# A planner that orders TensorE's work: a dearer change to "other" products, and wider bounds on their credit

## The chip, the cores and the metric

The kernel runs on one core of one Trainium2 chip. The metric is the device time of one execution in microseconds; lower is better. Times before the change: 2020.59, 2020.89 and 2028.12 us, median 2020.89 us. Besides these there is one profiled execution with its trace.

## The reference, cut to what matters

One block over a sequence of 2048 tokens with 512 features: six modulation rows from a condition vector, 32-head attention with heads of 16 features, then a mixer block (a token shift between two 512x512 products, and a two-layer MLP of 1792 hidden features).

```python
mod = (silu(c) @ w_mod).reshape(1, 6, 1, -1)          # sa, ca, ga, sb, cb, gb
h = layernorm(x) * (1 + ca) + sa
qkv = h @ wqkv                                          # q, k, v of 32 heads, 16 features each
p = softmax(q @ k.T * 16 ** -0.5)                       # 2048 x 2048 for each head
x = x + ga * ((p @ v) @ wo)
h = layernorm(x) * (1 + cb) + sb
# B: gelu(layernorm(h) @ w1), four feature groups shifted by +1, -1, +2, -2 tokens, @ w2, + h = x1
#    x1 + gelu(layernorm(x1) @ w3) @ w4
x = x + gb * B(h)
```

## The kernel before, in words

The kernel splits float32 operands in high and low parts, so a product of two matrices is three matmuls (lines 355, 357 and 359, the helper `mm3`). The attention is cut in 64 units: 4 chunks of 512 query tokens by 16 pairs of heads. A unit has 16 steps `s`, one for each 128 keys; each step has two rows `x = 2s` and `2s + 1`, one for each head of the pair.

TensorE has three kinds of work while the attention runs, and they use the array in three shapes:

- **rows** (mode "r"): one matmul of scores (`sc`, line 1036) beside one matmul of maxima (`mb`, line 1020), each on 64 of the array's 128 rows. ScalarE takes the exponential of `sc` (line 1032), VectorE the maximum of `mb` (line 1016), `LEAD` = 24 steps ahead. Each of the two needs a PSUM bank.
- **columns** (mode "c"): the probabilities times V (`pv`, lines 1113 and 1110), four matmuls side by side on 32 columns each. Line 1110 needs the low half of the probabilities, which GpSimd makes at line 1087.
- **other products** (mode "o"): the products of the whole array: q, k and v ahead of their use, and for each finished chunk wo, w1, w2, w3 and w4 with their transposes. Generators (`tail`, `o_fin` and others) yield one matmul at a time with its cost.

The order of all engines' instructions is fixed when the program is built. A planner, `Sched`, keeps a clock for each engine (`T["P"]` for TensorE) and adds estimated costs to it; the chip then executes each engine's list in order, and semaphores make it wait where an operand is late. The main loop (from line 1667) chooses again and again among rows, columns and other products:

- After a burst of up to `GRP` = 3 rows it works out `slack`: how long TensorE may do something else before the rows' banks and VectorE's or ScalarE's queue call for the next row. If at most `BACK` = 150 ns are left, the next row comes.
- Otherwise, with `CMIN` = 4 or more columns ready (or fewer that fit), columns come. Else other products run, one by one, until the clock reaches `stop`, which is now plus `slack`.
- Other products live on a **credit**. Each row adds half of `budget(s)`, at most up to `CTOP`; each product's cost is taken off. They run while the credit is over zero, or over `-OVER` while one of them holds a PSUM bank open. Over `CHIGH` they go on after `stop`, and a row does not start a burst. After each row the credit is lifted to `-OWE` if it is lower.
- `budget(s)` steers by a table, `DUES`, of how many us of other products are to be done by a step: 270.0 by step 505, 395.7 by step 765, 527.8 by step 1012, for instance.
- A change of mode costs `SWITCH` = 95 ns on the planner's clock, and `ENTER` = 107 ns more when rows are entered.

Chunks set what other products there are: the tail of a chunk can start only when the chunk's last unit is done, and the wo products wait for that.

Of the kernel before, what the change touches and what calls it, by code (L numbers as in the profile page):

```python
# [21 lines left out]
P = 128  # L22
# [25 lines left out]
TOLE = {"A": 500.0, "D": 500.0, "G": 800.0}  # L48
AGE = 0.2
DEBT = 3000.0  # L50
START, OVER = 1000, 1500
CROW, CCOL, CIN, CMID, COUT = 232.0, 230.0, 105.0, 95.0, 95.0
CFILL = 200.0
NSM = 7
# [28 lines left out]
XB = 4  # L83
SWITCH, ENTER = 95.0, 107.0
EARLY, STAY, BACK, GRACE = 300.0, 300.0, 150.0, 0.0
OWE, CTOP = 500.0, 5000.0
CHIGH, CMIN, CMOST, PTLOW, PLAG = 2500.0, 4, 6, 2, 1


class Sched:  # L90
# [14 lines left out]
    def to(self, mode):  # L105

        if self.mode != mode:
            self.T["P"] += SWITCH + (mode == "r") * ENTER
            self.mode = mode

    def now(self):
# [215 lines left out]
def kernel(ctx, tc, A_x, A_wqkv, A_wo, B_w1, B_w2, B_w3, B_w4, c, w_mod, out):  # L327
# [83 lines left out]
    sch = Sched()  # L411
# [509 lines left out]
    def drain(flag):  # L921
        while flag not in done:
            sch.step()

    def load_rows(t, src, pr, cs, to):
        for i in range(3):
            sch.dma(dma.dma_start, t[i + 1::4, to].bitcast(F32), src[2 * pr * DH:(2 * pr + 2) * DH, i, cs])
# [144 lines left out]
    def p_low(s):  # L1072

        p = pt[s].rearrange("p j n -> p (j n)")
        o, i = p.bitcast(F16)[:, 0::2], p.bitcast(U16)[:, 0::2]
        ready = e_exp.pop(s) + XX
        g, a = [max(sch.T[e], ready) for e in "GA"]
        if g > a + LACT:

            def half(h):  # L1080
                c = slice(h * CH, (h + 1) * CH)
                e_low[s] = XP["A"] + sch.crit("A", 690, ready, partial(act.activation, o[:, c], i[:, c], AF.Copy, scale=0.5))
            half(0)
            e_low[s] += 690 + 480
            second.append(partial(half, 1))
        else:
            e_low[s] = XP["G"] + sch.crit("G", 1345, ready, lambda: pool.tensor_scalar(  # L1087
                o, i, 0.5, 1.0, op0=OP.mult, op1=OP.mult))
# [38 lines left out]
    def ac_copy():  # L1127
        u, e = acs.pop()
        if u:
            drain(("of", u - 1))  # L1130
        ac = at.tile([P, CH], F32, name="ac", tag="ac", bufs=1)
        acc = pv.pop(u)
        e = sch.crit("A", cA(), e + PX, lambda: act.activation(ac, acc, AF.Copy))
        v_free[0] = e + XP["A"]
        sch.add(o_fin(u, ac, e + XP["A"]), 0)
# [439 lines left out]
    def budget(s):  # L1575
        if s < 0:
            return 800.0
        return min(BTOP, max([BLOW] + [(1000.0 * w - sch.spent) / (d - s) for d, w in DUES if d > s]))
# [5 lines left out]
    def before(s):  # L1584

        nu, r = divmod(s + 32, 16)
        if r == 0 and 0 < nu < NU:
            asked.append(nu)
        if asked:
            ci, pr = units[asked[0]]  # L1590
            keys = [("kq", pr // 4)] + [("q", pr // 8)] * (ci > 0)
            if r >= UWAIT:
                for key in keys:
                    drain(key)
            if all(key in done for key in keys):
                load_unit(asked.pop())
        if s in VAT:
            i = VAT.index(s)
            for kt in range(4 * i, 4 * i + 4):
                while kt not in near and ("vk", 0, kt) not in done:  # L1600
                    sch.step()
                if kt not in near:
                    sch.dma(dma.dma_start, vst[i][:, kt % 4], Vs[0, :, kt])
        if s == NS - 12:
            done.add("keys")
        if s == -12:
            unit_tiles(at, 2, dve, pool)
# [18 lines left out]
    def cols():  # L1626
        n, t = 0, sch.T["P"] + (sch.mode != "c") * SWITCH
        for y in pvs[:CMOST]:
            if n and y[0] % NKT == 0 and not y[1]:
                break  # L1630
            if col_at(y) > t + 20:
                break
            t += CCOL
            n += 1
        return n

    def fillers():
        for e in "ADG":
            sch.misc(e, max(sch.T["P"], sch.T[e]) + TOLE[e])

    def do_cols(n):
        sch.to("c")
        for y in pvs[:n]:
            if not y[1]:
                e_hi.pop(y[0])
            pv_part(*y)
        del pvs[:n]

    def do_row(x, t):
        sch.T["P"] = t  # L1650
        sch.to("r")
        late = sorted(e_exp)
        one_row(x)
        for q in late:
            if 2 * q < x - 2 * PLAG:
                p_low(q)
# [3 lines left out]
    while x < end or pvs or acs:  # L1660
        if acs:
            ac_copy()
        can = x < end
        if can:
            s, i = divmod(x, 2)
            if x == LENDS:
                sch.most = MOST
            if i == 0 and seen != s:
                seen = s
                before(s)  # L1670
                if s >= 0 and s % 16 == 0:
                    drain(("shift", s // 16))
            can = i or s < 0 or bool(pts)
        now, row, slack = sch.T["P"], False, LATE
        if can:
            need = (s >= 0) + (s + LEAD < NS)
            sch.flush(need)
            free = sorted(sm.t)
            one = free[need - 1 + 2 * (s < 0)]
            if one >= LATE:  # L1680
                one = free[need - 1]
            enter = (sch.mode != "r") * (SWITCH + ENTER)
        else:
            for q in sorted(e_exp):
                p_low(q)
            while second:
                second.pop(0)()
        nc_ = cols()
        if can:
            if sch.mode == "r" and burst < GRP:  # L1690
                slack = one - now
                row = slack <= STAY
            else:
                st = one
                for k in range(2, GRP + 1):
                    if need * k <= len(free) and free[need * k - 1] < LATE:
                        st = max(st, free[need * k - 1] - (k - 1) * CROW)
                dry = sch.T["D"] if s + LEAD < NS else sch.T["A"]
                slack = max(st, dry - CROW - PX - EARLY) - enter - now
                row = slack <= BACK and (sch.mode == "r" or sch.credit < CHIGH and not (nc_ >= CMIN and len(pts) <= PTLOW))  # L1700
        if not row:
            n = 0
            if nc_ >= CMIN or nc_ and slack >= nc_ * CCOL + (sch.mode != "c") * SWITCH:
                do_cols(nc_)
                n = nc_
            else:
                stop = now + max(slack, 0.0) + GRACE
                while (sch.T["P"] < stop or sch.credit > CHIGH) and sch.credit > (-OVER if sch.open else 0.0) and sch.one():
                    n += 1
            if not n:  # L1710
                if not can or one - enter > now + 100.0:
                    sch.T["P"] = now + 50.0
                else:
                    row = True
        if row:
            do_row(x, max(now, one - enter))
            burst = 1 if enter else burst + 1
            x += 1
            sch.credit = max(min(sch.credit + budget(s) / 2, CTOP), -OWE)
        fillers()  # L1720
        if tp[0] is None and x >= 2 * (NS // NC + TPO) and (x >= 2 * (NS // NC + TPL) or all(key in done for key in KEYS)):
            for key in KEYS:
                drain(key)
            qpx.close()
            tpx = ExitStack()
            tp[0] = tpx.enter_context(tc.tile_pool(name="tp", bufs=1, side="right"))
# [43 lines left out]
```

## Time and profile before

| What | Value |
|---|---|
| profiled execution: its own time | 2020.83 us |
| profiled execution: span from first to last instruction | 2019.0 us |
| mean granted TensorE clock | 0.992 |
| first and last matmul of scores | 96.02 and 1858.85 us |
| busy share: TensorE (PE) / VectorE (DVE) / ScalarE (ACT) / GpSimd (POOL) | 97% / 83% / 74% / 82% |
| instructions of the maxima at line 1016, mean | 2048, 683 ns |

In the profile PE is TensorE's matmuls and PEld its weight loads; DVE, ACT and POOL are VectorE, ScalarE and GpSimd. Matmuls are pipelined and their ends are modelled, so two that overlap by their durations may still be as close as they can be: pauses of TensorE are read from start to start. A table of stretches shows the busy us of each engine with the number of instructions in parentheses.

### The profile page before, as it was taken

To read this page: it belongs to the slowest core of one execution; us is meant where nothing else is said; L and a number is where in the kernel's file an instruction comes from. 1 tells how busy PE (TensorE), PEld (TensorE's weight loads), DVE (VectorE), ACT (ScalarE), POOL (GpSimd) and SP (SyncE) were. 2 spreads that over 40 slices of the span, in tenths; PEclk is the share of its full clock that TensorE was granted. 3 is DMA by queue.
4 is the path that set the end of the run, shared out by engine and by line. 5 is a ranking of instruction groups with operands and counts; after the bars stand their busy time and mean duration, and the time that the engine had idled before them with its cause. 6 is when DMAs were issued, how large, how long until landed. Compare 5 with 4: busy or idle time off the path is not lost.

```text
span 2019.0 us, 42344 instructions
## 1 busy us (share of the span) xinstructions
PE 1958.0 (97%) x14480; PEld 1133.0 (56%) x14480; DVE 1676.2 (83%) x3010; ACT 1495.4 (74%) x3113; POOL 1652.2 (82%) x1585
## 2 busy tenths in 40 slices
PE   7999999999999999999999999999999999998899
PEld 4655665554455555554455555555555555553798
DVE  7878888888988888889889988889998888883643
ACT  5376888888978877778787867777787777778443
POOL 6377999999989888889889988888899988887532
PEclk8999999999999999999999999999999999999999
DMA  5665878777523343435234243335333334342332
GB/s 181 203 200 164 243 230 262 253 224 258 183 86 110 114 135 123 132 111 157 77 103 143 86 142 95 115 105 195 87 102 126 106 118 135 110 133 82 141 152 89
DMA packets 233083, 293.24 MB, mean 145 GB/s; under 512 B 125876, under 2 KB 178052, under 8 KB 216580
## 3 DMA queue, kind: packets, MB, share of 16 engines
q1 hardware_dynamic: 232868, 290.53, 45.3%
q8 instruction: 115, 1.88, 0.4%
q14 instruction: 100, 0.82, 0.1%
HBM read 225.81 MB, written 62.91 MB: 143 GB/s over the span
## 4 chain that ended last, share of the span: by engine, by line
PE 76%; DVE 13%; ACT 5%; POOL 2%; issue 2%; DMA 1%; SPq 1%; POOLq 0%; ACTq 0%; DVEq 0%
PE mb L1020 14%; PE sc L1036 11%; PE pv L1113 10%; DVE mx L1016 9%; PE w L355 8%; PE w L359 7%; PE w L357 7%; PE pv L1110 7%; ACT pt L1032 2%; POOL pt L1087 1%; PE ot L1145 1%; PE v L355 1%; PE xT L1223 1%; PE q L355 1%; PE v L357 1%
## 5 line engine op out<-in xcount | busy, mean ns | idle before, releaser
L1016 DVE TENSOR_REDUCE mx<-mb 128x1 f32<-128x512 f32 x2048 | 1295.7, 683 | 160.9 <-PE mb L1020 126.2
L1087 POOL TENSOR_SCALAR pt<-pt 128x1024 f16<-128x1024 uint16 x964 | 1281.3, 1362 | 126.1 <-ACT pt L1032 122.7
L1032 ACT ACTIVATE pt<-sc 128x512 int32<-128x512 f32 x2048 | 1100.0, 608 | 312.3 <-PE mb L1020 228.3
L1020 PE MATMUL mb<-kst,qtl 64*128 64x512 f32 x2048 | 733.5, 448 | 22.1 <-DVE mx L1016 7.9
L1036 PE MATMUL sc<-qtl,kst 64*128 64x512 f32 x2048 | 709.5, 441 | 6.1 <-DMA qtl<-nm 2.3
L1020 PEld LDWEIGHTS mb<-kst,qtl 64*128 64x128 f32 x2048 | 343.5, 192 | 196.8 <-DVE mx L1016 69.7
L1036 PEld LDWEIGHTS sc<-qtl,kst 64*128 64x128 f32 x2048 | 334.5, 185 | 137.6 <-issue 48.1
L1113 PE MATMUL pv<-pt,vst 128*32 128x512 f16 x4096 | 362.5, 393 | 0.2
L1110 PE MATMUL pv<-pt,vst 128*17 128x512 f16 (+1 forms) x2048 | 215.5, 399 | 4.0 <-POOL pt L1087 4.0
L1113 PEld LDWEIGHTS <-vst 128*32 128x32 bf16 x4096 | 116.5, 94 | 117.5 <-issue 67.2
L355 PE MATMUL w<-A,wr 128*128 128x256 f32 (+2 forms) x576 | 174.6, 303 | 2.0 <-ACT pt L1032 1.3
L1447 POOL TENSOR_TENSOR g<-xs,g 128x256 fp32r<-128x256 f32 (+2 forms) x144 | 103.0, 716 | 86.1 <-ACT g L1446 83.9
L357 PE MATMUL w<-A,wr 128*128 128x256 f32 (+2 forms) x576 | 171.9, 298 | 0.5 <-DVE A L345 0.3
L359 PE MATMUL w<-A,wr 128*128 128x256 f32 (+2 forms) x576 | 171.8, 298 | 0.0
L1110 PEld LDWEIGHTS <-vst 128*17 128x17 f16 (+1 forms) x2048 | 54.0, 90 | 144.2 <-issue 135.1
L355 PEld LDWEIGHTS w<-A,wr 128*128 128x128 f32 x576 | 110.1, 191 | 30.4 <-issue 16.7
L359 PEld LDWEIGHTS w<-A,wr 128*128 128x128 f32 x576 | 109.9, 191 | 22.7 <-issue 22.7
L357 PEld LDWEIGHTS w<-A,wr 128*128 128x128 f32 x576 | 110.0, 191 | 20.6 <-issue 19.3
L355 PE MATMUL w<-wr,g 128*128 128x512 f32 x288 | 120.8, 419 | 0.7 <-ACT g L1446 0.6
L359 PE MATMUL w<-wr,g 128*128 128x512 f32 x288 | 119.1, 413 | 0.2 <-POOL g L1447 0.2
L357 PE MATMUL w<-wr,g 128*128 128x512 f32 x288 | 118.5, 412 | 0.0
L1443 ACT ACTIVATE sq<-w 128x256 f32<-128x256 f32 (+2 forms) x144 | 56.2, 391 | 56.6 <-PE w L359 54.6
(150 smaller groups left out, 2119.1 us busy)
## 6 DMA issues: line engine op xcount, KB each, us to landing
wr<-Ws SPq DMA_DIRECT2D x80, 1024.0 KB
kst<-Ks SPq DMA_DIRECT2D x189, 256.0 KB
vst<-Vs SPq DMA_DIRECT2D x252, 192.0 KB
qtl<-Qs SPq DMA_DIRECT2D x192, 64.0 KB
Vs<-vt SPq DMA_DIRECT2D x32, 384.0 KB
Ws<-wq SPq DMA_DIRECT2D x40, 256.0 KB
Ws<-wst SPq DMA_DIRECT2D x40, 256.0 KB
wst<-in_B_w_dram SPq DMA_DIRECT2D x36, 256.0 KB
```

Source lines behind the costliest of these rows:

```text
L355: te.matmul(o, lh, rh, start=first, stop=False)
L357: te.matmul(o, lh, rl, start=False, stop=False)
L359: te.matmul(o, ll, rh, start=False, stop=last)
L1016: end = sch.crit("D", 605, e + PX, lambda: dve.reduce_max(mxs[u][:, j, g, c:c + 1], b, axis=AX.X))
L1020: return ready, lambda: te.matmul(b, lhs, kst[u % 3][r, c * CH:(c + 1) * CH], start=True, stop=True), after
L1032: ea = sch.crit("A", 480, e + PX, lambda: act.activation(pt[s][:, j], b, AF.Exp))
L1036: return ready, lambda: te.matmul(b, kst[u % 3][r, kt * P:(kt + 1) * P], qst[u][r], start=True, stop=True), after
L1087: e_low[s] = XP["G"] + sch.crit("G", 1345, ready, lambda: pool.tensor_scalar(o, i, 0.5, 1.0, op0=OP.mult, op1=OP.mult))
L1110: te.matmul(acc[r:r + n, :], v[:, (kt + i) % 4, c - n:c].bitcast(F16), pt[s + i].bitcast(F16)[:, j, 0::2], start=False, stop=kt == NKT - 2 ...
L1113: te.matmul(acc[r:r + 32, :], v[:, kt % 4, r:r + 32], pt[s].bitcast(F16)[:, j, 1::2], start=kt == 0, stop=False, skip_group_check=True)
L1443: sch.chain(("A", cA(n), lambda: act.activation(sq, b, AF.Square, scale=2.0)), ("D", cD(n), cube), ("A", cA(n), lambda: act.activation(sq, ...
L1447: ("G", cG(n), lambda: pool.tensor_tensor(lo, xs, hi, op=OP.subtract)), (None, 0, end), bank=b)
```

## The change

The planner now counts 202 ns instead of 95 ns for each change to other products (rows have always cost 202, columns still cost 95). `OVER` goes from 1500 to 3000 ns, `OWE` from 500 to 1500, `CTOP` from 5000 to 7000 and `CHIGH` from 2500 to 6500. A condition with a new constant `OMIN` = 0 stands ahead of the loop that runs other products. `START`, which only the function `fill` reads, goes; nothing calls `fill`. No instruction's shape, tile or engine is changed by the diff itself.

```diff
-START, OVER = 1000, 1500
+OVER = 3000.0
...
-OWE, CTOP = 500.0, 5000.0
-CHIGH, CMIN, CMOST, PTLOW, PLAG = 2500.0, 4, 6, 2, 1
+OWE, CTOP, OMIN = 1500.0, 7000.0, 0.0
+CHIGH, CMIN, CMOST, PTLOW, PLAG = 6500.0, 4, 6, 2, 1
...
     def to(self, mode):
         if self.mode != mode:
-            self.T["P"] += SWITCH + (mode == "r") * ENTER
+            self.T["P"] += SWITCH + (mode != "c") * ENTER
             self.mode = mode
...
                 do_cols(nc_)
                 n = nc_
-            else:
+            elif slack >= OMIN or sch.mode == "o" or sch.credit > CHIGH:
                 stop = now + max(slack, 0.0) + GRACE
                 while (sch.T["P"] < stop or sch.credit > CHIGH) and sch.credit > (-OVER if sch.open else 0.0) and sch.one():
                     n += 1
```

## The prediction

> **What bounds the kernel now.** I read the page's totals first, then a table of stretches for the whole attention, then the waits, and then short pieces of the timeline.
>
> ```profile
> span 2019.0 us, 42344 instructions
> PE 1958.0 (97%) x14480; PEld 1133.0 (56%) x14480; DVE 1676.2 (83%) x3010; ACT 1495.4 (74%) x3113; POOL 1652.2 (82%) x1585
> 96.00:1859.00 1763.00, 1731.94 (x13299) 950.61 (x13297) 1523.29 (x2713) 1389.53 (x2895) 1543.01 (x1434) 1.00 0.46 145
> DVE mx L1016 <- PE mb L1020: 126.2, 270, 2.2
> DVE mx L1016 <- PE sc L1036: 28.6, 53, 2.2
> PEld mb L1020 <- DVE mx L1016: 69.7, 183, 2.1
> PEld mb L1020 <- ACT pt L1032: 44.8, 120, 1.4
> ```
>
> The attention is the stretch from 96 to 1859 us. TensorE looks 98% busy in it (1731.94 of 1763.00), while VectorE and GpSimd stand at 86 and 88%. But the waits go both ways: VectorE's maxima wait 126.2 + 28.6 = 154.8 us for rows, and the weight loads of the next maxima wait 69.7 + 44.8 = 114.5 us for a bank to come free. So neither engine is simply the bound. TensorE comes back to the rows too late in some rounds and too early in others, and between them it pays for changing shape. That price is in the starts of one lump of other products, with the work on either side:
>
> ```profile
> 992.77 0.42 PE L1113 MATMUL pv<-pt,vst 128*32 128x512 f16 x4
> 993.13 0.50 PE L355 MATMUL wo<-wr,A 128*128 128x512 f32 x1
> 993.46 0.39 PE L357 MATMUL wo<-wr,A 128*128 128x512 f32 x1
> 993.69 0.39 PE L359 MATMUL wo<-wr,A 128*128 128x512 f32 x1
> ...
> 995.53 0.39 PE L357 MATMUL wo<-wr,A 128*128 128x512 f32 x1
> 995.85 0.50 PE L1020 MATMUL mb<-kst,qtl 64*128 64x512 f32 x1
> ...
> 996.75 0.41 PE L1110 MATMUL pv<-pt,vst 128*17 128x512 f16 x4
> 996.99 0.49 PE L1113 MATMUL pv<-pt,vst 128*32 128x512 f16 x4
> ```
>
> Inside the lump starts are 0.23 us apart (993.46 to 993.69). From the last column to the first product are 0.36, from the first product to the second 0.33, from the last product to the first row 0.32. Columns run at full pace after their first group (996.75 to 996.99 is 0.24). So a lump of other products pays twice on entry, about 0.10 each, and the planner of before counts it once.
>
> How often: in the timeline of TensorE between the first and the last score I count 558 entries to other products, 708 to rows and 634 to columns. The first and last of the 558 begin with
>
> ```profile
> 98.03 0.39 PE L355 MATMUL v<-wp,hT 128*128 128x256 f32 x1
> ...
> 1850.24 0.66 PE L1145 MATMUL ot<-ident,ac 128*128 128x128 f32 x4
> ```
>
> The last view is the pace by stage. The count of line 1036 in a stretch is its number of rows; the second fence has line 355 alone, a third of the other products' matmuls.
>
> ```profile
> 504.00:545.00 41.00, 23.56 (x64) 10.75 (x65) 1.00 0.49 150
> 573.00:636.00 63.00, 23.74 (x68) 11.06 (x66) 1.00 0.29 90
> 746.00:913.00 167.00, 66.66 (x193) 31.71 (x193) 1.00 0.42 136
> 936.00:978.00 42.00, 22.82 (x66) 10.67 (x65) 1.00 0.33 91
> 1005.00:1069.00 64.00, 24.54 (x67) 11.07 (x65) 0.97 0.34 106
> 1207.00:1397.00 190.00, 75.27 (x225) 36.14 (x223) 1.00 0.39 123
> 1444.00:1506.00 62.00, 23.30 (x66) 10.83 (x65) 1.00 0.31 93
> ```
>
> ```profile
> 504.00:545.00 41.00, 0.00 (x0) 0.00 (x0) 1.00 0.49 150
> 573.00:636.00 63.00, 11.74 (x36) 6.82 (x36) 1.00 0.29 90
> 746.00:913.00 167.00, 35.99 (x108) 20.52 (x108) 1.00 0.42 136
> 1207.00:1397.00 190.00, 40.41 (x117) 22.04 (x117) 1.00 0.39 123
> 1816.00:1859.00 43.00, 1.66 (x4) 0.75 (x4) 0.96 0.32 102
> ```
>
> Three paces stand out. At the end of a chunk there are no other products (x0 at 504 to 545), and a row takes 41/64 = 0.64 us. Amid a chunk it takes 357/418 = 0.85 us. Just after a chunk's end (573, 1005 and 1444) it takes 189/201 = 0.94 us, though products are no denser there: 36/68 = 0.53 of line 355 a row, against 225/418 = 0.54 amid chunks.
>
> **The change part by part.**
>
> *The dearer entry.* No instruction is added. The planner's clock moves 0.107 us more at each entry, so the loop stops a lump that much earlier by true time: 558 x 0.107 = 59.7 us over the run. Two things follow. Rows come back up to 59.7 us earlier in sum, out of the 154.8 us for which VectorE waits on them. And 59.7 us of other products lose their place, about a quarter to a half of a matmul a lump. The table of dues still asks for the same total, so they must run elsewhere, and on TensorE they cost what they cost before. If they lengthen lumps that are entered anyway, the two cancel: 0. If they fill time in which TensorE now stands before a full bank (114.5 us, enough to hold them), the whole 59.7 is gained. If they need lumps of their own, of about 3 matmuls of 0.23 = 0.69 us, these are 87 more entries at 0.20, a loss of 17.5. I take 0, with the ends -59.7 and +17.5, because full lumps on TensorE are the nearest row: 0.85 us a row amid a chunk is set by what TensorE must do.
>
> By the Trainium skill, page "TensorEngine Tiling (Array Packing)", section "Key Properties", a change of tiling mode drains TensorE. That makes one pause for each change; the second pause, inside the lump (0.33 against 0.23), is not in it. By the rule alone the added 0.107 would count a pause that does not exist, and the sum would go to its upper end, 17.5 us dearer; the row shows that it exists.
>
> *The ceiling, 2500 to 6500, and the cap, 5000 to 7000.* By the dues between steps 505 and 765 a row brings (395.7 - 270.0)/260/2 = 0.242 us of credit. In the 64 rows without products the credit must run to the cap: 5.0 us need 21 rows, 7.0 need 29. Then the wo products come free, and everything over the ceiling is forced out in one lump: 2.5 us before, 0.5 us after. That is the lump of the timeline above, 11 matmuls from 993.13 to 995.85, and VectorE stands idle under it; the same comes at the other two ends:
>
> ```profile
> 996.39 1.89 DVE L1016 TENSOR_REDUCE mx<-mb 128x1 f32<-128x512 f32 x3 [2.18 <-PE sc L1036]
> 565.06 1.89 DVE L1016 TENSOR_REDUCE mx<-mb 128x1 f32<-128x512 f32 x3 [2.22 <-PE mb L1020]
> 1441.30 1.29 DVE L1016 TENSOR_REDUCE mx<-mb 128x1 f32<-128x512 f32 x2 [1.70 <-PE sc L1036]
> ```
>
> The idle time sums to 6.1 us. The most that a softer start could give is the whole excess after the three ends, 189 - 201 x 0.854 = 17.3 us; the rest of it may be the new chunk's own VectorE work. I take the middle, -12 (ends -17 and 0, the latter if the forced work only moves by some rounds).
>
> *The wider band before a chunk's end.* Up to 4.0 us more of other products may be owed when a chunk ends, and they then run in the stretch that has none now. There a row takes 0.64 us, of which TensorE's own part is 0.23 for the row, 3 groups of columns for 4 rows at 0.23 (0.17 a row), and, in rounds of three rows, a third of two entries, 0.20 + 0.09 (0.10): 0.50. So 0.14 a row is spare, 9 us in 64 rows, which is cover for 4.0 us, unless its own entries use it up. Three times 4.0 is 12; I take half, -6 (ends -12 and 0).
>
> *The debt, `OVER` and `OWE`.* An open bank may be finished down to -3.0 us of credit instead of -1.5, and up to 1.5 us of the debt is kept instead of 0.5. It matters only where the credit is near zero. A bank is held open less long, but a pause in products follows. Nothing in the trace prices it; by one row's pace I bound it at 1 us either way a chunk, 4 in all, and take 0.
>
> *The end.* Up to 4.0 us of products may be left when the last row is done, and then nothing hides them. But 1816 to 1859 has 4 matmuls of line 355 in 43 us: products have run out before the end. I take +1 (0 to +4).
>
> *`OMIN` and `START`.* With slack under zero outside mode "o", a row would have been chosen unless columns are due (they go first) or the credit is at the ceiling, and that is admitted by the condition itself. `fill` has no caller. Both 0.
>
> The sum: 0 - 12 - 6 + 0 + 1 = -17 on the profiled execution's 2020.83 us, so 2004 us. That execution lies 0.06 under the median, which changes nothing.
>
> **The rivals.**
>
> *Slower: the ceiling becomes the rule.* Each lump loses 0.107 us of its slack, so slack alone may no longer cover the dues. Then the credit climbs to 6.5 us after the first chunk and stays. Each round then forces out only what its three rows bring, 3 x 0.242 = 0.73 us, about 3 matmuls, so the displaced 59.7 us come in lumps of their own: +17.5, and no relief after chunks; 2038 us. It decides when products that fit into slack fall under 0.242 us a row. For it: the rounds amid a chunk have both kinds of waits and little spare. Against: 114.5 us of bank waits are spare.
>
> *No change.* Work moved by 4 us is only moved: 59.7 against 59.7, forced lumps come some rounds later, VectorE idles then. For it: TensorE's work is the same to the matmul. Time 2020, within 2011 to 2030.
>
> *Much faster.* Half of the 59.7 us go into the bank waits: -30 beside -17; 1974 us. For it: the planner's order would at last fit the engine's pauses. Against: the same work must fit into the same rounds.
>
> **How the numbers follow.** A difference of 0.5%, 10 us, is about what a measurement of this kernel can tell from no change. The forecast, 1990 to 2010, has 0.45; much faster 0.10; no change 0.25; slower 0.20. So faster has 0.55, same 0.25, slower 0.20. The range reaches from the much faster case, 1976, to just under the slower one, 2036; each side leaves out about one in ten. The forecast's own range is 1990 to 2010.
>
> **What would show it.** The 11-matmul lumps of wo after a chunk's end should be 4 or fewer, without VectorE's idle 2 us; rows in the three stretches after it should take under 0.90 us. VectorE's wait for rows should be under 154.8 us. If entries to other products rise from 558 to 620 or more, the slower rival is at work. If the waits shrink on one side and grow as much on the other, it is no change. The prediction is wrong if the pace amid chunks, 0.85, moves by more than 0.02 a row: 1300 rows at that pace make it 26 us.

## The result, and the profile after

The changed kernel takes 2011.56 us (median of 5 runs, 2009.32 to 2012.32), the kernel before 2020.89 us (5 runs); the ratio is 0.9943 with a 95% interval of 0.9925 to 0.9961. The ratios in this document take in all runs, not the medians alone, whose quotient is 0.9954 here. So the change makes the kernel about half a per cent faster, which is little more than the prediction took to be measurable at all. The profiled execution took 2012.32 us, 8.5 less than that of before.

First the totals, the whole attention and the waits of the changed kernel, as shown of before:

```profile
span 2010.5 us, 42313 instructions
PE 1960.9 (98%) x14480; PEld 1131.9 (56%) x14480; DVE 1681.5 (84%) x3010; ACT 1483.1 (74%) x3087; POOL 1672.8 (83%) x1598
94.80:1849.30 1754.50, 1733.35 (x13301) 948.43 (x13300) 1524.77 (x2707) 1379.76 (x2872) 1564.77 (x1447) 1.00 0.46 145
DVE mx L1016 <- PE mb L1020: 112.8, 277, 2.0
DVE mx L1016 <- PE sc L1036: 21.0, 60, 1.4
PEld mb L1020 <- DVE mx L1016: 80.2, 231, 1.2
PEld mb L1020 <- ACT pt L1032: 29.2, 80, 1.0
```

The attention went from 1763.0 to 1754.5 us, which is the whole gain of the profiled execution. VectorE's wait for rows fell from 154.8 to 112.8 + 21.0 = 133.8 us. The weight loads' wait for banks fell slightly, from 114.5 to 80.2 + 29.2 = 109.4 us, and its longest single wait from 2.1 to 1.2 us.

TensorE did not change shape less often. Counted as before, between the first and the last score, the entries to other products rose from 558 to 617, those to rows from 708 to 717; columns have 633 (634). Of the 59 added entries, 41 are lumps of a single matmul (27 before, 68 now). Such a lump has no second matmul, and so only the first of the two pauses of 0.10 us that the prediction read from the starts. The added changes of shape thus cost about 9 us: 59 first pauses, 18 second ones, and 9 entries to rows at 0.20. The products done before the last row are some 2 us fewer. So the pauses of TensorE that are left over, its stalls, must have shrunk by about 8.5 + 9 - 2 = 16 us. This is an estimate. If one takes off the usual start-to-start time of each shape and each change of shape instead, what is left falls by 12 us. Either way more changes of shape were paid for with fewer stalls. The 21 us by which VectorE waits less for rows are idle time of another engine; they need not be the same.

Then the pace by stage, all of line 1036 first, line 355 alone in the second fence. The windows follow the same stages as before:

```profile
502.00:543.00 41.00, 23.54 (x65) 10.73 (x65) 1.00 0.49 152
571.00:635.00 64.00, 24.18 (x68) 10.72 (x66) 1.00 0.28 90
745.00:905.00 160.00, 66.46 (x195) 31.74 (x195) 1.00 0.37 121
931.00:978.00 47.00, 23.53 (x64) 10.73 (x65) 1.00 0.53 161
1003.00:1065.00 62.00, 23.73 (x66) 10.79 (x66) 1.00 0.31 93
1200.00:1385.00 185.00, 75.25 (x226) 36.65 (x225) 1.00 0.37 114
1438.00:1500.00 62.00, 23.13 (x66) 10.46 (x64) 1.00 0.30 93
```

```profile
745.00:905.00 160.00, 30.18 (x91) 17.02 (x90) 1.00 0.37 121
931.00:978.00 47.00, 2.56 (x6) 1.13 (x6) 1.00 0.53 161
1200.00:1385.00 185.00, 35.08 (x99) 18.62 (x99) 1.00 0.37 114
1806.00:1849.00 43.00, 7.72 (x23) 4.32 (x23) 1.00 0.36 122
```

Amid a chunk a row takes 345/421 = 0.82 us instead of 0.85, with 190/421 = 0.45 of line 355 a row instead of 0.54: products moved out of there. Some appear in the stretch at the second chunk's end, which now takes 47/64 = 0.73 us a row instead of 0.64. More run in the last rows of the third and the fourth chunk: line 355 comes 33 times instead of 16 in the last 64 rows of the third, and 23 times instead of 4 in the last 43 us of the fourth. So the faster pace amid a chunk is for the most part the absence of products that run later in the same chunk. Whole chunks hold nearly the same products (line 355 differs by at most 3), and by the starts of their first scores they take 448, 435, 436 and 435 us instead of 449, 433, 441 and 440. The gain arises in the last two chunks, at about 0.01 us a row.

In the three stretches after a chunk's end a row takes 188/200 = 0.94 us, exactly as before.

### The profile page after: what moved, and what is told of

Read it like the earlier page. It is cut to its first block, busy times and chain, and to the rows that moved or that the text cites. A ratio compares the mean times of both kernels' runs of the same rounds, so it can differ in the third digit from the quotient of the medians.

```text
span 2010.5 us, 42313 instructions
## 1 busy us (share of the span) xinstructions
PE 1960.9 (98%) x14480; PEld 1131.9 (56%) x14480; DVE 1681.5 (84%) x3010; ACT 1483.1 (74%) x3087; POOL 1672.8 (83%) x1598
## 4 chain that ended last, share of the span: by engine, by line
PE 79%; DVE 10%; ACT 4%; DMA 2%; POOL 2%; issue 1%; SPq 1%; POOLq 0%; ACTq 0%; DVEq 0%
PE mb L1020 15%; PE sc L1036 13%; PE pv L1113 11%; PE w L355 8%; PE w L357 8%; PE w L359 7%; PE pv L1110 7%; DVE mx L1016 6%; ACT pt L1032 2%; PE ot L1145 1%; POOL pt L1087 1%; PE xT L1223 1%; PE v L355 1%; PE mr L660 1%; PE v L359 1%
## 5 line engine op out<-in xcount | busy, mean ns | idle before, releaser
L1016 DVE TENSOR_REDUCE mx<-mb 128x1 f32<-128x512 f32 x2048 | 1296.5, 683 | 139.8 <-PE mb L1020 112.8
L1087 POOL TENSOR_SCALAR pt<-pt 128x1024 f16<-128x1024 uint16 x977 | 1301.2, 1366 | 103.7 <-ACT pt L1032 99.9
L1020 PEld LDWEIGHTS mb<-kst,qtl 64*128 64x128 f32 x2048 | 342.8, 193 | 183.1 <-DVE mx L1016 80.2
L1437 DVE SCALAR_TENSOR_TENSOR sq<-sq,w 128x256 f32<-128x256 f32 (+2 forms) x144 | 60.4, 420 | 47.0 <-ACT sq L1443 44.2
```

Source lines behind the costliest of these rows:

```text
L1016: end = sch.crit("D", 605, e + PX, lambda: dve.reduce_max(mxs[u][:, j, g, c:c + 1], b, axis=AX.X))
L1020: return ready, lambda: te.matmul(b, lhs, kst[u % 3][r, c * CH:(c + 1) * CH], start=True, stop=True), after
L1437: dve.scalar_tensor_tensor(sq, sq, 1.0 / GELU_A, b, op0=OP.add, op1=OP.mult)
```

## The experiments

The change has two parts of weight: the dearer entry and the higher ceiling with its cap. A third, the debt, was expected to do nothing. Theory 1 says that the entry alone brings the gain (bookkeeping), theory 2 that the ceiling does (the wider band), theory 3 that each needs the other, and theory 4 that any new order of instructions moves the time by several us, so that the result is a draw. All ratios below are to the kernel before, run on the same chip.

### The dearer entry alone (e1_entry_only)

```diff
-            self.T["P"] += SWITCH + (mode == "r") * ENTER
+            self.T["P"] += SWITCH + (mode != "c") * ENTER
```

> The kernel before, with the dearer entry alone (202 instead of 95 ns for each change to other products); all credit bounds as before. Theory 1, bookkeeping: the whole gain of 9 us comes from a plan that knows the pause, so this is about 2012 us. Theory 2, the wider band: the entry alone gives nothing or costs, 2020 to 2030 us, because the displaced products are forced out at the low ceiling of 2500. Theory 3, both are needed: slower than before, 2025 us or more. Theory 4, the draw of the order: any change of the order moves the time by several us, so anything from 2010 to 2030.

Measured: 2022.61 us against 2022.86, ratio 0.9995 (0.9986 to 1.0004). Theory 1 as put falls: the entry alone does not bring the gain. It does not cost 0.2% either, as theory 3 had it. VectorE's wait for rows fell by 6.5 us, to 148.3 (in a profiled execution at a granted clock of 0.995, against 0.992 before):

```profile
DVE mx L1016 <- PE mb L1020: 125.5, 271, 3.5
DVE mx L1016 <- PE sc L1036: 22.8, 60, 1.7
```

while the entries to products rose from 558 to 593, and those of a single matmul from 27 to 51, which by the count above costs about 5 us. That the two cancel is argued from these sizes, not shown.

### The four bounds alone (e2_bounds_only)

```diff
-START, OVER = 1000, 1500
+START, OVER = 1000, 3000.0
-OWE, CTOP = 500.0, 5000.0
-CHIGH, CMIN, CMOST, PTLOW, PLAG = 2500.0, 4, 6, 2, 1
+OWE, CTOP = 1500.0, 7000.0
+CHIGH, CMIN, CMOST, PTLOW, PLAG = 6500.0, 4, 6, 2, 1
```

> The kernel before, with the four credit bounds alone (OVER 3000, OWE 1500, CTOP 7000, CHIGH 6500); the entry stays at 95 ns. Theory 1, bookkeeping: no change, 2019 to 2022 us. Theory 2, the wider band: the whole gain, about 2012 us. Theory 3, both needed: less than half of the gain, 2017 to 2021 us. Theory 4: anything from 2010 to 2030 us, not the sum of its parts.

Measured: 2023.73 us, ratio 1.0005 (0.9995 to 1.0015). Theory 2 as put falls too: the bounds alone bring nothing. With both parts at nothing and the whole at 0.9943, theories 3 and 4 were left.

### The ceiling and the cap alone (e3_ceiling_only), and the debt alone (e4_debt_only)

The first sets `CTOP` 7000 and `CHIGH` 6500, the second `OVER` 3000 and `OWE` 1500; all else is as before.

> The kernel before, with CHIGH 6500 and CTOP 7000 alone. Theory 2, the wider band: as with all four bounds, about 2012 us, and the row pace in the stretches at the chunks' ends above 0.64 us because products are left for them. Theory 1: 2020 us. Theory 4: off from the run with four bounds by several us although the debt hardly matters.

> The kernel before, with OVER 3000 and OWE 1500 alone. All theories but the fourth: within 4 us of the kernel before, 2017 to 2025 us, since the credit is seldom near zero. Theory 4: several us off, either way.

Measured: the ceiling alone 2015.06 us, ratio 0.9963 (0.9951 to 0.9976); the debt alone 2031.02 us, ratio 1.0040 (1.0027 to 1.0053). The ceiling gives something without the debt, and the debt takes as much again. That the debt should cost 8 us was expected by theory 4 alone.

### Entry with ceiling (e5_entry_ceiling), and entry with debt (e6_entry_debt)

These are the changed kernel with one pair of bounds taken back: `OVER` 1500 and `OWE` 500 in the first, `CHIGH` 2500 and `CTOP` 5000 in the second.

> The changed kernel with the debt as before (OVER 1500, OWE 500): the dearer entry with CHIGH 6500 and CTOP 7000. If the parts add up (entry 0.9995, ceiling 0.9963), a ratio near 0.996 to the kernel before. If entry and ceiling need each other and the debt plays no part, 0.994, as the whole change. If the whole change is a lucky order, anything from 0.993 to 1.004.

> The changed kernel with CHIGH 2500 and CTOP 5000 as before: the dearer entry with the debt. If the parts add up (entry 0.9995, debt 1.004), near 1.0035. If the ceiling is what the gain hangs on, 1.000 to 1.004. If debt and dearer entry are what fit each other, 0.995.

Measured: 2010.75 us, ratio 0.9933 (0.9918 to 0.9948), and 2017.45 us, ratio 0.9969 (0.9961 to 0.9978). Entry and ceiling without the debt bring all that the whole change brings. With the dearer entry the debt lowered the ratio by 0.0026 (0.9995 to 0.9969) where it had raised it by 0.0040 with the cheap one. An effect that changes its sign like this is not one that these runs can call the debt's own. The first range, 0.993 to 1.004, was no test of a lucky order, since it holds nearly every outcome.

### Orders without a meaning (e7_after_ceiling6600, e8_before_grace5)

The changed kernel with `CHIGH` 6600 instead of 6500, and the kernel before with `GRACE` 5 instead of 0.

> The changed kernel with CHIGH 6600 instead of 6500, which should mean nothing to the mechanism but gives another order. If the gain is one of the settings, 0.994 again, within 0.002. If it is the draw of the order, off by 0.003 or more.

> The kernel before with GRACE 5 ns instead of 0: a lump of other products may run 5 ns longer. It has no meaning of its own but gives another order. If orders of the same settings agree, 1.000 within 0.002. If the draw of the order counts, off by 0.003 or more, either way.

Measured: 2018.79 us, ratio 0.9981 (0.9971 to 0.9991), and 2036.15 us, ratio 1.0057 (1.0040 to 1.0075). So 5 ns of grace made the kernel before slower by 0.57%, as much as the whole change gained. This order alone is worth that much, and the interval of a ratio, which comes from repeated runs of one order, does not contain it. The ceiling of 6600 moved the changed kernel by 0.0038, which is just over the limit set for the draw.

The run with the ceiling of 6600 shows something of its own. Its last score stands 11 us earlier than that of the changed kernel, and its end 3 us later. The rows are, in this order, those of the changed kernel and of the kernel with 6600: all scores, then line 355 after the last one.

```profile
L1036 PE MATMUL sc<-qtl,kst x2048: 383/395/793, 94.9 to 1849.3; 64*128 64x512 f32 x187
...
1849.30:2010.50 161.20, 88.98 (x255) 49.33 (x255) 0.97 0.36 133
```

```profile
L1036 PE MATMUL sc<-qtl,kst x2048: 383/395/793, 95.1 to 1838.1; 64*128 64x512 f32 x187
...
1838.00:2014.00 176.00, 98.10 (x282) 54.57 (x282) 0.98 0.39 145
```

27 more matmuls of line 355 (282 against 255; each stands for one of line 357 and one of line 359 as well) run where no row hides them, and the stretch after the last score takes 176 us instead of 161. This order made the attention shorter by leaving work for the end.

### The same four settings in another order (e9_entry_grace5, e10_ceiling_grace5, e11_after_grace5)

To tell settings from draws, `GRACE` 5 went into the entry-only kernel, the bounds-only kernel and the changed kernel as well.

> The dearer entry with all bounds as before, and GRACE 5 ns: another order of the entry-only kernel (ratio 0.9995). If the dearer entry is worth something on average and the draw of the order comes on top, 0.995 to 1.001, below the 1.000 to 1.006 seen with the cheap entry and the low ceiling. If only the draw counts, 0.994 to 1.006 with no side preferred.

> The four wider bounds with the cheap entry, and GRACE 5 ns: another order of the bounds-only kernel (ratio 1.0005). If the higher ceiling is worth something on average, 0.995 to 1.001. If only the draw counts, 0.994 to 1.006 with no side preferred.

> The changed kernel with GRACE 5 ns: another order of the whole change. If entry and ceiling add up, 0.992 to 0.997. If the whole change was a lucky order, about 1.000 or more.

Measured: 0.9996 (0.9987 to 1.0004), 0.9987 (0.9978 to 0.9996) and 0.9935 (0.9922 to 0.9947; 2010.27 us). The first two lie in the ranges of both readings and decide nothing by themselves; the third speaks against a lucky order. All orders that differ in nothing but the debt, the grace or 100 ns of ceiling, side by side:

| Entry | Ceiling | Ratios | Mean |
|---|---|---|---|
| 95 | 2500 | 1 (before), 1.0040, 1.0057 | 1.0032 |
| 202 | 2500 | 0.9995, 0.9969, 0.9996 | 0.9987 |
| 95 | 6500 | 1.0005, 0.9963, 0.9987 | 0.9985 |
| 202 | 6500, 6600 | 0.9943, 0.9933, 0.9935, 0.9981 | 0.9948 |

Within a line the orders differ by 0.0027 to 0.0057. The dearer entry lowers the mean by 0.0045 at the low ceiling and by 0.0037 at the high one; the higher ceiling lowers it by 0.0047 and 0.0039. These means rest on three or four orders each. The runs hold a closer comparison: pairs that differ in one setting and in nothing else (the condition with `OMIN` aside, which by the code does nothing).

| Entry 95 to 202, with | Ratio | VectorE's wait for rows, us |
|---|---|---|
| all else as before (e1) | 1 to 0.9995 | 154.8 to 148.3 |
| the debt (e4, e6) | 1.0040 to 0.9969 | 161.4 to 146.9 |
| the ceiling (e3, e5) | 0.9963 to 0.9933 | 154.0 to 134.5 |
| all four bounds (e2, the change) | 1.0005 to 0.9943 | 156.7 to 133.8 |
| grace 5 (e8, e9) | 1.0057 to 0.9996 | 167.3 to 141.3 |
| all four bounds, grace 5 (e10, e11) | 0.9987 to 0.9935 | 157.4 to 140.0 |

| Ceiling and cap raised, with | Ratio | VectorE's wait for rows, us |
|---|---|---|
| all else as before (e3) | 1 to 0.9963 | 154.8 to 154.0 |
| the debt (e4, e2) | 1.0040 to 1.0005 | 161.4 to 156.7 |
| the dearer entry (e1, e5) | 0.9995 to 0.9933 | 148.3 to 134.5 |
| entry and debt (e6, the change) | 0.9969 to 0.9943 | 146.9 to 133.8 |

The dearer entry lowers the ratio in all six pairs, by 0.0047 on average, and by nearly as much at the low ceiling (0.0046) as at the high one (0.0048). The ceiling lowers it in all four, by 0.0040. So each setting gains by itself, and the two add up: theory 3 falls. Theory 4 holds for the size of any single comparison, but not for the whole change: its four orders lie under all three of the cheap entry with the low ceiling. The entry alone looked like nothing because the one pair that was run first is the weakest of the six, and the bounds alone because the debt came with them. By what way each setting shortens the attention is not settled by this: VectorE's wait falls in every pair, but not in step with the time.

### An entry counted too dear (e12_after_entry309)

```diff
-            self.T["P"] += SWITCH + (mode != "c") * ENTER
+            self.T["P"] += SWITCH + ((mode != "c") + (mode == "o")) * ENTER
```

> The changed kernel with an entry to other products counted at 309 ns, 107 more than the pauses that the trace shows. If an earlier return to the rows is what pays, it gets faster still, 0.988 to 0.992, with VectorE's wait for rows below that of the changed kernel. If the truth of the cost is what pays, it is slower than the changed kernel, 0.996 to 1.005. In both cases the entries rise above 621 and products may be left for the end, which makes the stretch after the last row longer than 161 us.

Measured: 2024.05 us, ratio 0.9999 (0.9989 to 1.0008), 0.0056 above the changed kernel and beyond the spread of its line in the table. By the expectations this speaks against an earlier return as such. VectorE's wait for rows is 140.2 us, over the changed kernel's 133.8, the entries to products rise to 659, and the last score is at 1854.2 us of a span of 2023.8, so that 170 us follow it instead of 161:

```profile
DVE mx L1016 <- PE mb L1020: 121.2, 256, 4.3
DVE mx L1016 <- PE sc L1036: 19.0, 54, 1.2
L1036 PE MATMUL sc<-qtl,kst x2048: 383/395/792, 92.9 to 1854.2; 64*128 64x512 f32 x187
```

It is one order, and the loss is not spread over the run. From the first to the 513th score, the first chunk, it takes 467 us against 448 of the changed kernel. The other three chunks take 1294 us against 1306, with 19 fewer of line 355, and as many more come after the last score (274 against 255). Why the first chunk suffers was not traced. So the fall back agrees with a cost that should be the true one, and it does not show it.

## Why the prediction was right or wrong, point by point

The prediction was 2004 us, faster; measured were 2011.56, faster, and inside the range of 1976 to 2036. The narrower range of the forecast itself, 1990 to 2010, was missed by 1.6 us, and 2011.56 also lies at the edge of the range that was given to no change. The sign and the place (the attention) are right. The sum was twice too large: -17 against -8.5 in the profiled executions. But this is one order against one order, and the kernel before is the fastest order of its settings. By the means of the table the change is worth 0.9948 - 1.0032 = -0.0084, which is -17 us. That this is the size of my sum is luck: a term put at nothing (the entry) brought about half of it, and terms put at -18 brought about the other half.

**The dearer entry, taken as 0 with ends -59.7 and +17.5.** The three outcomes were put as alternatives, and two of them happened together. The displaced products took lumps of their own: 59 more entries, where 87 were the upper end. Most of these were lumps of one matmul, not of the three that I had taken. I had also taken 0.23 us for every matmul; products of 256 columns, nearly half of them, start 0.12 us apart, so 0.107 us is about a whole one. And stalls went away, by the estimate above 12 to 16 us in the whole change. The term is -0.0005 in the first pair and -0.0047, about -9 us, on average over the six. So 0 was the wrong size: the step that failed is that displaced products would only lengthen other full lumps, because TensorE's work sets the pace. The test that I gave for the slower rival was wrong: entries of 620 or more would show it at work. They rose to 617 here and to 641 with the ceiling at 6600, and both are faster than before; entries are not a measure of the time unless the stalls are counted with them.

**The second pause on entry.** The Trainium skill's page "TensorEngine Tiling (Array Packing)", section "Key Properties", says that a change of tiling mode drains TensorE. By one pause for each change the sum would have been dearer. No run went that way; the entry at 202 lowered the ratio in all six pairs. That the second pause exists can be read in the whole attention before: the median time from a lump's first product to its second is 0.34 us where 512 columns are streamed, against 0.23 further on (223 lumps), and 0.22 against 0.12 for 256 columns (202 lumps). For 128 columns it is less, 0.165 against 0.110. That knowing this pause is why the dearer entry pays is argued, with the single order at 309 beside it.

**The ceiling, -12 by a softer start of a chunk.** The lump did what I said, and the pace did not. After the second chunk's end the 11 matmuls of wo in one piece became pieces of 6, 1 and 2, and VectorE's idle 2.18 us became at most 0.50. Beside the wo products of the other two ends it became at most 0.74, from 2.22 and 1.70. (After the first end the changed kernel has 1.60 us of it 7 us ahead of its first wo product, under a wait of TensorE for a transfer of V.) A lump of 6 is still more than the 4 that I had named as the sign. Starts on TensorE, then on VectorE, in the changed kernel:

```profile
991.91 0.50 PE L355 MATMUL wo<-wr,A 128*128 128x512 f32 x1
992.24 0.39 PE L357 MATMUL wo<-wr,A 128*128 128x512 f32 x1
...
993.17 0.40 PE L359 MATMUL wo<-wr,A 128*128 128x512 f32 x1
993.50 0.50 PE L1036 MATMUL sc<-qtl,kst 64*128 64x512 f32 x1
...
995.21 0.51 PE L355 MATMUL wo<-wr,A 128*128 128x512 f32 x1
995.64 0.50 PE L1020 MATMUL mb<-kst,qtl 64*128 64x512 f32 x1
...
997.34 0.50 PE L357 MATMUL wo<-wr,A 128*128 128x512 f32 x1
997.68 0.40 PE L359 MATMUL wo<-wr,A 128*128 128x512 f32 x1
998.00 0.49 PE L1036 MATMUL sc<-qtl,kst 64*128 64x512 f32 x1
```

```profile
994.06 1.89 DVE L1016 TENSOR_REDUCE mx<-mb 128x1 f32<-128x512 f32 x3 [0.26 <-PE mb L1020]
996.18 1.89 DVE L1016 TENSOR_REDUCE mx<-mb 128x1 f32<-128x512 f32 x3 [0.23 <-PE sc L1036]
998.57 1.89 DVE L1016 TENSOR_REDUCE mx<-mb 128x1 f32<-128x512 f32 x3 [0.50 <-PE mb L1020]
```

But the three stretches after the chunks' ends still take 0.94 us a row (188/200), where I had put under 0.90 as the sign. The failed step is that their excess over 0.85 came from the forced lump. The lumps that I named cannot be it: the stretches begin at 573, 1005 and 1444 us, and the lumps with VectorE's idle time are over by 566, 996 and 1442. The excess of 17.3 us was read in windows that leave out its supposed cause. In the rows that do hold the lumps, the first 32 or so after each end, the time fell from 80 to 77 us together, with 11 of line 355 instead of 22. What the excess in the later stretches comes from was not tried.

**The wider band, -6.** Products did move to a chunk's end (6 of line 355 in 931 to 978, none before; 0.73 us a row instead of 0.64), and still more in the last rows of the third and the fourth. Amid the chunks the pace fell from 0.85 to 0.82. That move of 0.03 is beyond the 0.02 a row by which I said the prediction would be wrong. As a saving it would be some 40 us, and the kernel gained 8.5: the windows lost products (0.54 to 0.45 of line 355 a row), which come back at the chunk's end, and the sign was badly chosen. This term and the softer start together were -18; the ceiling's four pairs give 0.0026 to 0.0062, on average 0.0040, about 8 us. So the two terms were over-sized twofold. How the 8 us divide between them is open.

**The debt, 0.** Neither shown nor refuted: its four pairs give +0.0040, +0.0042, -0.0026 and +0.0010. The bound of 4 us was too narrow, since the first two are over 8 us.

**The end, +1.** The stretch after the last score went from 160 to 161 us. But its bound of +4 was no bound: with a ceiling of 6600 it is 176 us.

**`OMIN` and `START`, 0.** Argued from the code; no run was made for them.

**What the prediction did not have at all** is the draw of the order. The range held the time, but "a difference of 0.5%" was put as about what a measurement can tell from no change, and here two orders of the same settings differ by as much as 0.57%.

## What to carry to other kernels

When a planner fixes the order of instructions, a change of its costs or bounds is also a new draw of the order: compare several orders of each setting (a nudge without a meaning makes one) before believing a difference of half a per cent. Pairs that differ in one setting, over several combinations of the others, tell most: six pairs of one sign say what no single pair of this size can. Before you call a faster stage a gain, compare the work in it. Read a cost that the planner leaves out from start to start, as with the second pause of 0.10 us on entry; counting it helped in all six pairs, and counting 107 ns more gave the gain back in the one order that was run. Count changes of shape and stalls together, since one can pay for the other, and look at what is left after the last hidden work before praising a shorter stage.

## What the runs showed that I had not expected

Five ns of grace in the plan moved the kernel before from 2023.32 us (the median on that chip) to 2036.15 us, with the same number of matmuls. In the profiled executions, of which this one had a granted clock of 0.987 against 0.992, the attention runs from 94.8 to 1874.9 us instead of 96.0 to 1859.0, and VectorE waits 132.6 + 34.7 = 167.3 us for rows instead of 154.8:

```profile
L1036 PE MATMUL sc<-qtl,kst x2048: 383/396/793, 94.8 to 1874.9; 64*128 64x512 f32 x187
DVE mx L1016 <- PE mb L1020: 132.6, 269, 2.5
DVE mx L1016 <- PE sc L1036: 34.7, 62, 2.5
```

The wait of VectorE for rows is longest in this slowest order and shortest, 133.8 us, in the changed kernel, but it is no measure of the time. With the entry at 202, low bounds and 5 ns of grace it is 141.3 us, 13.5 less than before, and the attention is 2 us longer than before (98.3 to 1863.3 us). The changed kernel with 5 ns of grace and the one with the entry at 309 have the same wait (140.0 and 140.2 us), and the second takes 14 us more.
